# Seven PSUM banks instead of three for one more attention head, and for the norm before it

## The chip, the cores and the metric

One core of one Trainium2 chip runs the whole program. The metric is device time in microseconds (us) of one execution. Engines are named as in the profile: PE (TensorE, matmuls), PEld (its weight loads), DVE (VectorE), ACT (ScalarE), POOL (GpSimd), SP (the queue that issues the DMAs). PSUM is the memory that PE writes its results to. This kernel cuts it into eight tiles of 128 x 512 float32, called banks below: four named `pm`, three named `ps`, one named `po`.

## The reference

```python
# attention, 4 batches x 8 heads, 576 positions, 64 wide, mask by blocks of 64
scores = scale * q @ k.T; scores = where(block_i >= block_j, scores, -1e9)
attn = exp(scores - max); attn = attn / (sum + 1e-9)
x = (attn @ v), heads side by side                      # 2304 tokens x 512
# gated feed-forward ("MoE 1"), 512 -> 1536 -> 512
xn = x / sqrt(mean(x * x) + 1e-6) * rms_g
x = (silu(xn @ w_gate) * (xn @ w_val)) @ w_out
# mixture of 8 experts ("MoE 2"), 512 -> 1024 -> 512, with a weight P for each token and expert
P = exp(x @ gate - max); 8 rounds of scaling its rows and columns
out = sum over e of P[:, e] * (relu(x @ w1[e]) @ w2[e])
```

## The kernel before

Heads are numbered 0 to 31 (head i is head i % 8 of batch i // 8), so head 8 opens the second batch and "the second batch's second head" is head 9. The Python code first writes a graph of operations, in program order; `Graph.emit` then plans twelve orders for all engines with estimated durations and keeps the best. What the program order fixes for good is the use of buffers: each `Ring` hands out its tiles in turn, and an operation on a newly drawn tile waits for everyone who used that tile before.

`attention` runs heads as a software pipeline. Its step i makes, in turn, the scores of head i and the second half of head p = i - 1:

- `s_a` to `s_d` (matmuls L504): four score blocks, one bank each; DVE takes negated row maxima (L513, combined in L554), ACT the exponentials (L520). The longest rows span two banks, so `s_c` and `s_d` are both held until the exponentials after `s_d`.
- `s_norm` (DVE L671 and L672, ACT L679 or DVE L681): scales the rows by one over their sums.
- `t_x0` to `t_x3` (heads from 7 on): PE transposes the weights (L689) into one bank each; ACT (L695) and DVE (L696) take a high and a low part out.
- `pv_a` to `pv_d` (L729): products with v into the single `po` bank, the last 64 columns into the bank of `t_x3`; ACT (L754) copies one half to a `tm` tile, DVE (L757) adds the other.

Heads 0 to 6 use another form of the second half, also with four banks a head. So each head draws eight banks from the ring `ps_ring[0]`.

After the last head of a batch comes its norm. `rms_a` sums squares with ten tiny matmuls (L792) into a first bank; DVE takes the inverse root there (L796 to L802) and spreads it on a diagonal (L809); PE broadcasts it (L818) into a bank for 512 tokens and one for the last 64. For the first batch these banks are read straight by `rms_b`: eight multiplications on DVE (L877, four of 512 and four of 64 columns), each followed by a copy to a high part (ACT, L294) and a subtraction for the low part (POOL or DVE, L307). Their `tm` tiles come from a ring of three, shared with `pv_d`. For later batches the banks are copied out first (L827).

Only a batch that has its norm can feed MoE 1 (matmuls L959 up, L1015 down, on the `pm` banks). `attention` is a generator: at each `yield` the caller adds some groups of MoE 1 to the graph, four groups for the first batch's tokens at the first `yield`. PE then mixes their matmuls with the attention of later batches.

Banks pass from one use to the other so. At first `PS0`, a ring of seven, serves attention: ps0, pm0, ps1, pm1, ps2, pm2, pm3. Heads 0 to 8 with their scores and heads 0 to 7 with their second halves draw 68 times from it. Then `PS` (three banks) serves attention, and `PM` (four) serves MoE 1; `PS.after = PM.after = PS0` makes the first draws of both wait for the users of `PS0` on the same tile. The first batch's norm draws its three banks from `PM`.

Other helpers in the rows: L294, L298 and L300 are copies that split off high parts, L307 the subtractions for low parts, L350 to L356 the conversion of weights, L474 a step of loading a head, L662 the end of a head in the other form, L765 and L777 the squares and their sum.

Of the kernel before, what the change touches and what calls it, by code (L numbers as in the profile page):

```python
# [197 lines left out]
def t_act(n, psum=False, ap=0):  # L198
    if ALONE:
        return (165 if psum else 190) + 0.845 * n + 144 * ap  # L200
    return (50 if psum else 92) + n / 1.2 + 90 * ap
# [17 lines left out]
def t_v2(n):  # L219
    return Both(150 + n / 1.92) if ALONE else 120 + n / 0.96  # L220
# [10 lines left out]
def t_f32(n):  # L231
    return 2 * max(n / 1.2, 107.0) + 2
# [3 lines left out]
def tile_attn_moe_moe2(ctx: ExitStack, tc: tile.TileContext, qT, kT, vP, wg, wv, wo, rg, gw, w1, w2, ident_d, mq_d, mk_d, bm_d, out):  # L236
    nc = tc.nc
    B, H, D, S = qT.shape
# [18 lines left out]
    def tiles(pool, n, shape, dt, name):  # L257
        return [pool.tile(shape, dt, name=f"{name}{i}") for i in range(n)]
# [17 lines left out]
    PM = Ring(tiles(psp, 4, [128, 512], F32, "pm"))  # L276
    PS = Ring(tiles(psp, 3, [128, 512], F32, "ps"))
# [4 lines left out]
    ps_ring = [PS0]  # L282
# [119 lines left out]
    def A(*a, **k):  # L402
        k.setdefault("prio", 1.0)
        o = G.op(*a, **k)
        att_ops.append(o)
        return o
# [40 lines left out]
    def att_load(i):  # L447
        b, h = divmod(i, H)
        Rqa, Rqb, Rka, Rkb, Rrq = (*b0_rings, RQ0) if i < H else (QA, QB, KA, KB, RQ)
        qb, kb = Rqb.next(), Rkb.next()  # L450

        def load_two(b_, src):
            def ld():
                nc.sync.dma_start(out=b_()[0:64], in_=src[b, h])
                nc.sync.dma_start(out=b_()[64:128], in_=src[b, h])
            A("SP", 1200, ld, w=[b_], lat=2000)

        if H <= i < H + 2:

            clear = st["clear", i % 2] = qb.part()  # L460
            A("DVE", 300, lambda: nc.vector.memset(f32(qb()[96:128, :]), 0.0), w=[clear])
        qq, kk = Rrq.next(), Rrq.next()
        load_two(kk, kT)
        load_two(qq, qT)
        qa, ka = Rqa.next(), Rka.next()
        sc = 1.0 if i in NEW else scale
        copy(A, S, ka, kk, r=[kk], w=[ka])
        copy(A, S, lambda: qa()[:, PAD:640], qq, sc, r=[qq], w=[qa])
        copy(A, S, lambda: qb()[0:64, PAD:640], lambda: qq()[0:64], sc, r=[qq], w=[qb])
        minus(A, S, lambda: kb()[0:64], lambda: kk()[0:64], lambda: f32(ka()[0:64]), r=[kk, ka], w=[kb], margin=GAIN)  # L470
        if i in NEW:
            minus(A, S, lambda: qa()[64:128, PAD:640], lambda: qq()[64:128], lambda: f32(qa()[64:128, PAD:640]), r=[qq, qa], w=[qa], margin=GAIN)
        else:
            A("DVE", 120 + t_v1(S), lambda: nc.vector.scalar_tensor_tensor(  # L474
                out=qa()[64:128, PAD:640], in0=qq()[64:128], scalar=scale, in1=f32(qa()[64:128, PAD:640]), op0=ALU.mult, op1=ALU.subtract),
                r=[qq, qa], w=[qa])
        st["in", i] = (qa, qb, ka, kb)

    def att_open(i):
        b, h = divmod(i, H)  # L480
        st["m", i], st["sm", i] = MN.next(par=True), SM.next(par=True)
        st["P", i] = [p.next(par=True) for p in PP]
        if i not in NEW and i < H + 1:
            for t in (0, 3):
                p = st["P", i][t]
                A("POOL", 150, lambda p=p, t=t: nc.gpsimd.memset(p()[:, NKEY[t] :], 0.0), w=[p])
        if i in NEW:
            vx = st["vs", i] = VX.next()

            def ldv():  # L490
                nc.sync.dma_start(out=vx()[:, 0:4, D : 2 * D], in_=vP[b, h][:, 0:4])
                nc.sync.dma_start(out=vx()[64:128, 4, D : 2 * D], in_=vP[b, h][0:64, 4])

            A("SP", 1200, ldv, r=[vones], w=[vx], lat=2000)
            return
        vr, vs = RV.next(), VS.next()
        st["vs", i] = vs
        A("SP", 700, lambda: nc.sync.dma_start(out=vr(), in_=vP[b, h]), w=[vr], lat=2000)
        copy(A, 320, lambda: vs()[:, :, 0:D], vr, r=[vr], w=[vs])
        minus(A, 320, lambda: vs()[:, :, D : 2 * D], vr, lambda: f32(vs()[:, :, 0:D]), r=[vr, vs], w=[vs], margin=GAIN2)  # L500
# [281 lines left out]
    def rms_a(b):  # L782


        ring = PM if b == 0 else ps_ring[0]
        ss, ps, c = st.pop(("ss", b)), ring.next(), CL.next()
        V = nc.vector
        at = [min(128 * t, S - 128) for t in range(5)]

        def sums():  # L790
            for t in range(5):
                nc.tensor.matmul(out=ps()[:, t : t + 1], lhsT=ss()[:, at[t] : at[t] + 128], rhs=ones_t[:, 0:1], start=True, stop=True)  # L792

        def newton():
            m, t, y = ps()[:, 8:13], ps()[:, 16:21], c()
            V.tensor_scalar(out=m, in0=ps()[:, 0:5], scalar1=1.0 / DM, scalar2=1e-6, op0=ALU.mult, op1=ALU.add)  # L796
            V.tensor_scalar(out=t.bitcast(I32), in0=m.bitcast(I32), scalar1=1, scalar2=None, op0=ALU.logical_shift_right)
            V.tensor_scalar(out=y.bitcast(I32), in0=t.bitcast(I32), scalar1=-1, scalar2=0x5F3759DF, op0=ALU.mult, op1=ALU.add)
            for _ in range(3):
                V.tensor_tensor(out=t, in0=y, in1=m, op=ALU.mult)  # L800
                V.scalar_tensor_tensor(out=t, in0=t, scalar=-0.5, in1=y, op0=ALU.mult, op1=ALU.mult)
                V.scalar_tensor_tensor(out=y, in0=t, scalar=1.5, in1=y, op0=ALU.add, op1=ALU.mult)  # L802

        A("PE", 1200, sums, r=[ss, ones, mask], w=[ps], prio=0.0)
        A("DVE", 2500, newton, r=[ps], w=[c])
        dg = SS.next(par=True)
        for t in range(5):
            n = min(128, S - 128 * t)
            A("DVE", 63 + t_v2(n), lambda t=t, n=n: V.tensor_scalar_mul(  # L809
                out=dg()[:, 128 * t : 128 * t + n], in0=ident_t[:, 128 - n : 128], scalar1=c()[:, t : t + 1]), r=[c, ident], w=[dg], prio=0.9)  # L810
        spreads = []
        for o, n in ((0, 512), (512, S - 512)):
            y = ring.next()

            def spread(y=y, o=o, n=n):
                for k in range(0, n, 128):
                    w = min(128, n - k)
                    nc.tensor.matmul(out=y()[:, k : k + w], lhsT=ones_t, rhs=dg()[:, o + k : o + k + w], start=True, stop=True)  # L818

            A("PE", t_f32(n), spread, r=[dg, ones], w=[y], prio=0.0)  # L820
            spreads.append((o, n, y))
        if b == 0:
            st["y", b] = [(o, o + n, y) for o, n, y in spreads]
        else:
            ys = SS.next(par=True)
            for o, n, y in spreads:
                A("ACT", t_act(n, True), lambda o=o, n=n, y=y: nc.scalar.activation(  # L827
                    out=ys()[:, o : o + n], in_=y()[:, 0:n], func=AF.Copy), r=[y], w=[ys], prio=0.9)
            st["y", b] = [(0, S, ys)]
# [62 lines left out]
    def attention():  # L892

        att_init()
        att_load(0)
        att_open(0)
        A("SP", 300, lambda: nc.sync.dma_start(out=ident_t, in_=ident_d), w=[ident], lat=2000)
        A("SP", 100, lambda: nc.sync.dma_start(out=rg_t, in_=rg), w=[rgs], lat=2000)
        def nothing(i):
            pass  # L900

        old = ((t_x0, nothing), (t_x1, pv_a), (t_x2, pv_b), (t_x3, pv_c), (nothing, pv_d))
        new = ((st_a, nothing), (st_b, sv_a), (st_c, sv_b), (st_d, sv_c), (nothing, sv_d))
        for i in range(NH + 1):
            p = i - 1
            for s, (x, y) in zip((s_a, s_b, s_c, s_d, s_norm), new if p in NEW else old):
                if i < NH:
                    s(i)
                if p >= 0:
                    y(p)  # L910
                    x(p)
            if i + 1 < NH:
                att_load(i + 1)
                att_open(i + 1)
            if p >= 0:
                b, h = divmod(p, H)
                if h % 2:
                    sq_step(b, h // 2)
                if h == H - 1:
                    rms_a(b)  # L920
                    rms_b(b)
                    if b == 0:
                        ps_ring[0] = PS
                        b0_ops.update(*(x.users for x in (bm, vones, *VX, *M10, *SR, *RC, *RQ0)))
                    yield


# [768 lines left out]
```

## Time and profile before

| | |
|---|---|
| median of 3 runs | 2183.27 us (2181.48 to 2185.68) |
| profiled execution | 2186.54 us, of which the span from first to last instruction is 2184.8 us |
| mean granted clock of PE | 0.989 of full speed |
| busy share of the span | PE 98%, PEld 85%, DVE 64%, POOL 53%, ACT 44% |

The busy shares are means over phases with different limits: attention fills the first 470 us or so, and MoE 1 and 2 the rest. Attention of the second batch overlaps the first batch's MoE 1 from about 106 us on. A mean clock of 0.5 in a stretch is PE's lower level (1.2 GHz), 1.0 the higher (2.4 GHz).

### The profile page before, as it was taken

To read this page: it belongs to the slowest core of one execution; us is meant where nothing else is said; L and a number is where in the kernel's file an instruction comes from. 1 tells how busy PE (TensorE), PEld (TensorE's weight loads), DVE (VectorE), ACT (ScalarE), POOL (GpSimd) and SP (SyncE) were. 2 spreads that over 40 slices of the span, in tenths; PEclk is the share of its full clock that TensorE was granted. 3 is DMA by queue.
4 is the path that set the end of the run, shared out by engine and by line. 5 is a ranking of instruction groups with operands and counts; after the bars stand their busy time and mean duration, and the time that the engine had idled before them with its cause. 6 is when DMAs were issued, how large, how long until landed. Compare 5 with 4: busy or idle time off the path is not lost.

```text
span 2184.8 us, 31245 instructions
## 1 busy us (share of the span) xinstructions
PE 2145.4 (98%) x10974; PEld 1859.9 (85%) x10974; DVE 1402.8 (64%) x2396; ACT 967.2 (44%) x2118; POOL 1160.9 (53%) x1079
## 2 busy tenths in 40 slices
PE   8899999999999999999999999999999999999999
PEld 5677788888999998999999999899888888888887
DVE  6789887863633577555555555555676677767666
ACT  6888786661421543333343433433343333233332
POOL 6556446311522666665565565565465556465554
PEclk9799999999999999999999999999999999999999
DMA  5666667635775544555545555555666566556663
GB/s 158 191 192 215 214 201 242 196 128 185 241 248 203 209 177 175 193 183 178 174 174 185 182 183 185 187 181 175 208 202 194 201 202 200 197 200 205 193 201 116
DMA packets 160976, 419.20 MB, mean 192 GB/s; under 512 B 22298, under 2 KB 52826, under 8 KB 160820
## 3 DMA queue, kind: packets, MB, share of 16 engines
q1 hardware_dynamic: 160820, 417.22, 57.2%
q8 instruction: 86, 1.41, 0.3%
q14 instruction: 70, 0.57, 0.1%
HBM read 274.74 MB, written 141.08 MB: 190 GB/s over the span
## 4 chain that ended last, share of the span: by engine, by line
PE 83%; DVE 2%; ACT 1%; POOL 1%; issue 1%; POOLq 0%; DVEq 0%; ACTq 0%
PE ps L1359 25%; PE pm L1427 20%; PE pm L1584 11%; PE pm L959 9%; PE pm L1359 7%; PE pm L1015 5%; PE po L1584 3%; PE ps L689 1%; PE po L729 1%; PE ps L504 1%; PE po L974 0%; DVE qa L474 0%; DVE xs L307 0%; DVE mn L513 0%; DVE acc L1443 0%
## 5 line engine op out<-in xcount | busy, mean ns | idle before, releaser
L1359 PE MATMUL ps<-xs,w 128*128 128x384 f32 (+2 forms) x2478 | 505.5, 346 | 2.2 <-ACT t L1369 1.2
L1359 PEld LDWEIGHTS ps<-xs,w 128*128 128x128 f32 x2478 | 435.7, 188 | 46.4 <-ACT t L1369 1.9
L959 PE MATMUL pm<-x,w 128*128 128x512 f32 (+1 forms) x1440 | 341.2, 378 | 0.0
L1443 DVE SCALAR_TENSOR_TENSOR acc<-pm,Pm,acc 128x512 f32<-128x512 f32 x280 | 209.7, 750 | 162.2 <-PE pm L1427 159.0
L1427 PE MATMUL pm<-w,h 128*128 128x512 f32 x1152 | 279.1, 391 | 0.0
L959 PEld LDWEIGHTS pm<-x,w 128*128 128x128 f32 x1440 | 254.4, 190 | 28.3
L307 POOL TENSOR_TENSOR w<-raw,w 128x512 fp32r<-128x512 f32 (+1 forms) x163 | 195.0, 1206 | 105.0 <-ACT w L294 96.4
L1427 PEld LDWEIGHTS pm<-w,h 128*128 128x128 f32 x1152 | 210.0, 188 | 39.7
L1427 PE MATMUL pm<-w,x 128*128 128x512 f32 x768 | 186.8, 392 | 0.0
L307 POOL TENSOR_TENSOR h<-t,h 128x512 fp32r<-128x512 f32 (+1 forms) x64 | 80.1, 1251 | 182.4 <-ACT h L294 169.8
L1565 DVE TENSOR_TENSOR acc<-pm,acc 128x512 f32<-128x512 f32 x169 | 116.5, 690 | 81.1 <-PE pm L1584 80.4
L1427 PEld LDWEIGHTS pm<-w,x 128*128 128x128 f32 x768 | 143.1, 188 | 26.9
L1015 PE MATMUL pm<-h,w 128*128 128x512 f32 (+1 forms) x720 | 162.8, 375 | 0.0
L1015 PEld LDWEIGHTS pm<-h,w 128*128 128x128 f32 x720 | 131.1, 190 | 16.0
L1374 DVE TENSOR_TENSOR pad<-ps,pad 128x384 f32<-128x384 f32 (+2 forms) x127 | 66.3, 522 | 114.1 <-ACT pad L1369 72.0
L1359 PE MATMUL pm<-xs,w 128*128 128x256 f32 (+2 forms) x654 | 139.1, 336 | 0.0
L307 POOL TENSOR_TENSOR w<-pad,w 128x512 fp32r<-128x512 f32 x64 | 88.6, 1386 | 71.3 <-ACT w L294 71.3
L1584 PE MATMUL pm<-x,w 128*128 128x512 f32 x510 | 125.6, 389 | 0.5 <-DVE x L307 0.5
L1359 PEld LDWEIGHTS pm<-xs,w 128*128 128x128 f32 x654 | 112.2, 189 | 14.7
L307 POOL TENSOR_TENSOR x<-pad,x 128x512 fp32r<-128x512 f32 (+1 forms) x71 | 94.7, 1337 | 54.1 <-ACT x L294 54.1
L1369 ACT ACTIVATE pad<-ps 128x256 f32<-128x256 f32 (+2 forms) x115 | 55.0, 478 | 140.1 <-PE ps L1359 140.0
L1584 PEld LDWEIGHTS pm<-x,w 128*128 128x128 f32 x510 | 95.7, 188 | 20.7 <-DVE x L307 0.9
(365 smaller groups left out, 4140.6 us busy)
## 6 DMA issues: line engine op xcount, KB each, us to landing
raw<-w_dram SPq DMA_DIRECT2D x128, 256.0 KB, 3.0
w<-kg SPq DMA_DIRECT2D x48, 512.0 KB, 4.1
w<-kv SPq DMA_DIRECT2D x48, 512.0 KB, 3.5
w<-ko SPq DMA_DIRECT2D x48, 512.0 KB, 4.0
fa<-w SPq DMA_DIRECT2D x32, 512.0 KB, 4.3
fd<-w SPq DMA_DIRECT2D x32, 512.0 KB, 3.9
fc<-w SPq DMA_DIRECT2D x32, 512.0 KB, 2.9
sb<-w SPq DMA_DIRECT2D x32, 512.0 KB, 3.8
```

The source lines that it names most:

```text
L307: eng.tensor_tensor(out=out_(), in0=a(), in1=b(), op=ALU.subtract)
L504: nc.tensor.matmul(out=ps()[:, o : o + n], lhsT=a[:, 128 * t : 128 * t + 128], rhs=c[:, k0 : k0 + n], start=start, stop=stop)
L689: A("PE", 109, lambda: nc.tensor.transpose(out=ps()[:, o : o + 128], in_=p()[:, 128 * c : 128 * c + 128], identity=ident_t), r=[p, ident, ...
L959: nc.tensor.matmul(out=ps()[:, 0:n], lhsT=w()[:, a, 128 * k : 128 * k + 128], rhs=xv()[:, c, k, 0:n], start=k == 0 and (a, c) == (0, 0), s ...
L1015: nc.tensor.matmul(out=ps()[:, 0:n], lhsT=wos[q]()[:, a, 128 * m : 128 * m + 128], rhs=ht()[:, c, 0:n], start=q == 0 and (a, c) == (0, 0), ...
L1359: nc.tensor.matmul(out=bank()[:, 0:n], lhsT=w()[:, a, o + 128 * k : o + 128 * k + 128], rhs=views[p, q, i, k, c](), start=start and k == 0 ...
L1369: G.op("ACT", t_act(n, True), lambda: nc.scalar.activation(out=t()[:, 0:n], in_=bank()[:, 0:n], func=AF.Copy), r=[bank], w=[t])
L1374: G.op("DVE", t_v1(n), lambda: nc.vector.tensor_tensor(out=t()[:, 0:n], in0=bank()[:, 0:n], in1=t()[:, 0:n], op=ALU.add), r=[bank, t], w=[t])
L1427: nc.tensor.matmul(out=y(), lhsT=hs[f][half]()[:, a, o : o + 128], rhs=ws[f]()[:, c, :], start=f == 0 and (a, c) == (0, 0), stop=f == GF - ...
L1443: G.op("DVE", 63 + t_v1(512), lambda y=y, dst=dst, tt=tt, e=e: nc.vector.scalar_tensor_tensor(out=dst(), in0=wide(y()), scalar=Pm()[:, tt, ...
L1565: G.op("DVE", t_v1(N), lambda: nc.vector.tensor_tensor(out=dst(), in0=bank()[:, 0:N], in1=dst(), op=ALU.add), r=[bank, dst], w=[dst])
L1584: nc.tensor.matmul(out=bank()[:, 0:N], lhsT=w()[:, a, o : o + 128], rhs=ops[i][gi]()[:, c, 0:N], start=start and gi == 0 and (a, c) == (0, ...
```

## The change

`rms_a` draws its banks from whatever ring attention uses at the time, for the first batch too. The switch to three banks, and with it the first `yield`, moves from the end of the step with p = 7 to the end of the step with p = 8.

```diff
     def rms_a(b):
...
-        ring = PM if b == 0 else ps_ring[0]
+        ring = ps_ring[0]
         ss, ps, c = st.pop(("ss", b)), ring.next(), CL.next()
...
                     rms_a(b)
                     rms_b(b)
                     if b == 0:
-                        ps_ring[0] = PS
                         b0_ops.update(*(x.users for x in (bm, vones, *VX, *M10, *SR, *RC, *RQ0)))
+                    else:
+                        yield
+                elif p == H:
+                    ps_ring[0] = PS
                     yield
```

So after 68 draws the seven-bank ring goes on for eleven more: three for the norm, then the scores of head 9 in turn with the second half of head 8. Counted through the ring: norm pm2, pm3, ps0; `s_a` pm0, `t_x0` ps1, `s_b` pm1, `t_x1` ps2, `s_c` pm2, `t_x2` pm3, `s_d` ps0, `t_x3` pm0. Before the change these eight were ps0, ps1, ps2, ps0, ps1, ps2, ps0, ps1, and the norm had pm0, pm1, pm2. No instruction is added or taken away.

## Rows read from the trace of the kernel before

**Rows 1.** The page: busy tenths of PE and its clock in 40 slices.
```profile
PE   8899999999999999999999999999999999999999
...
PEclk9799999999999999999999999999999999999999
```
**Rows 2.** Busy time by stretch: PE, PEld, DVE, ACT, POOL, then clock and DMA.
```profile
86.50:106.50 20.00, 16.62 (x63) 14.13 (x62) 15.38 (x41) 15.90 (x39) 12.95 (x10) 0.50 0.60 204
...
106.00:215.00 109.00, 103.79 (x534) 85.06 (x532) 100.84 (x189) 93.41 (x233) 69.62 (x56) 0.96 0.63 199
215.00:230.00 15.00, 11.55 (x49) 9.59 (x48) 12.69 (x27) 6.55 (x18) 7.66 (x7) 0.77 0.72 249
230.00:470.00 240.00, 235.95 (x1257) 196.74 (x1256) 191.03 (x393) 183.65 (x469) 99.04 (x90) 1.00 0.61 198
```
**Rows 3.** PE in order of time: start, length, instruction, [idle before].
```profile
84.56 0.63 PE L504 MATMUL ps<-ka,qa 128*128 128x320 f32 x1 [2.49 <-DVE xx L757]
...
85.63 1.91 PE L689 MATMUL ps<-ident,p 128*128 128x128 f32 x8
...
88.74 0.79 PE L504 MATMUL ps<-ka,qa 128*128 128x512 f32 x1
...
90.18 0.26 PE L504 MATMUL ps<-ka,qa 128*128 128x64 f32 x1
...
90.98 1.05 PE L689 MATMUL ps<-ident,p 128*128 128x128 f32 x4
...
92.21 2.13 PE L792 MATMUL pm<-ones,ss 128*128 128x1 f32 x10
...
98.00 0.93 PE L689 MATMUL ps<-ident,p 128*128 128x128 f32 x2 [2.56 <-ACT p L679]
98.72 1.91 PE L818 MATMUL pm<-ss,ones 128*128 128x128 f32 x8
...
106.09 2.75 PE L959 MATMUL pm<-x,w 128*128 128x512 f32 x9
...
113.56 0.39 PE L729 MATMUL po<-pth,vs 128*128 128x512 f32 x1
...
209.19 1.17 PE L792 MATMUL ps<-ones,ss 128*128 128x1 f32 x10
```
**Rows 4.** DVE in order of time, the same stretch.
```profile
84.28 0.22 DVE L757 TENSOR_TENSOR xx<-ps,tm 64x64 f32<-64x64 f32 x1
...
94.37 0.17 DVE L796 TENSOR_SCALAR pm<-pm 128x5 f32<-128x5 f32 x1 [2.31 <-PE pm L792]
...
96.68 0.16 DVE L671 TENSOR_REDUCE rs<-sm 128x5 f32<-128x15 f32 x1
...
100.67 0.75 DVE L877 SCALAR_TENSOR_TENSOR tm<-xx,rgs,pm 128x512 f32<-128x512 f32 x1 [0.42 <-PE pm L818]
...
110.98 0.56 DVE L877 SCALAR_TENSOR_TENSOR tm<-xx,rgs,pm 128x64 f32<-128x64 f32 x2 [0.18 <-POOL x L307]
112.25 0.53 DVE L300 TENSOR_SCALAR qa<-rq 128x576 fp32r<-128x576 f32 x1 [0.71 <-PE ps L504]
...
113.37 4.08 DVE L300 TENSOR_SCALAR qb<-rq 64x576 fp32r<-64x576 f32 x1
```
**Rows 5.** ACT in order of time.
```profile
80.91 0.73 ACT L520 ACTIVATE p<-pm,mn 128x512 f32<-128x512 f32 x1
...
102.73 0.62 ACT L294 ACTIVATE x<-tm 128x512 fp32r<-128x512 f32 x1
...
109.25 0.60 ACT L754 ACTIVATE tm<-po 64x512 f32<-64x512 f32 x1
```
**Rows 6.** POOL in order of time.
```profile
89.04 1.43 POOL L777 TENSOR_TENSOR ss<-ss,tm 128x576 f32<-128x576 f32 x1 [1.06 <-DMA kv<-w]
...
103.43 1.27 POOL L307 TENSOR_TENSOR x<-tm,x 128x512 fp32r<-128x512 f32 x1 [0.64 <-ACT x L294]
...
115.84 1.29 POOL L356 TENSOR_TENSOR raw<-acc 128x512 int32<-128x512 int32 x1
```

## The prediction

> **What bounds the kernel now.** I read the page first: PE is at nine tenths or more in all slices but the first two, and only the second, which holds the place of the change, has a low clock [rows 1]. Then the busy time by stretch [rows 2]. From 230 us on PE is nearly gapless (235.95 of 240 us busy, full clock), so what happens there is paid in matmuls, and the change adds none. What it can move is the PE time lost before: the norm of the first batch (86.5 to 106.5 us, PE at the lower clock level throughout, 3.4 us idle), the overlap of the second batch's attention with MoE 1 (106 to 215 us, 5.2 us idle), and the wait for the second batch's norm (215 to 230 us, 3.45 us idle, mean clock 0.77). In that last stretch PE has run out of MoE work that may start, so a delay or gain of the second batch's attention reaches the end of the kernel as it is. The overlap stretch is DVE's more than PE's: DVE 100.84 of 109 us.
>
> Last I followed each engine in order of time through the norm [rows 3 to 6]. The reader should see two things. First, a bank wait: head 9's `s_b` starts at 84.56, 2.49 us late, released by the DVE addition at 84.28 that ends head 7 [rows 3, 4]; it draws the tile that head 7's `t_x3` had. Over the 20 us from 86.5 PE's clock is at the lower of its levels (0.50) [rows 2]. Second, the norm is one long chain with attention squeezed between its links: POOL completes the sum of squares at 89.04 + 1.43 = 90.47 [rows 6], PE starts the tiny matmuls only at 92.21, DVE gets them at 94.37, PE broadcasts at 98.72, DVE multiplies at 100.67, ACT copies at 102.73, POOL subtracts until 103.43 + 1.27 = 104.70, and MoE 1 starts at 106.09.
>
> **The change, part by part.** The instructions are the same; only the tiles differ, and so the waits.
>
> *Head 9's first two blocks.* `s_b` moves to pm1, last used by head 8's `s_d`, whose exponentials follow those of `s_c` (80.91 + 0.73) [rows 5]: some 82 us instead of 84.56. `s_a`, which before ran earlier than `s_b`, must now wait for pm0, which head 8's `s_c` holds to 81.64. So the 2.49 us wait goes, but the next PE work, the eight transposes at 85.63 [rows 3], needs head 8's scaled rows and no bank. I count 0 for this; bounds 0 and -2.5 us.
>
> *Head 9's last blocks and head 8's `t_x2` get the norm's banks.* This is the dear part. `s_c` (88.74 before) must wait until DVE is done with pm2 (94.37 to about 96.7); `t_x2` (90.98 before) until the four 512-column multiplications have read pm3; `s_d` (90.18 before) until the four 64-column ones have read ps0, and their last pair ends at 110.98 + 0.56 = 111.54 before [rows 3, 4]. Queued behind `s_d` are head 9's maximum, its exponentials, `s_norm` (96.68 before), its transposes (98.00 before), and head 10's `s_a`, whose ps0 is `s_d`'s. PE's part of all this runs after MoE 1 has begun, no longer in time that PE would lose anyway. The three 512-column matmuls between 88.74 and 90.18 take 0.48 us each at the lower level, so 0.24 at the higher, 0.47 ns a column. Pushed out are `s_c`, `s_d` (2 x 576 columns), head 10's `s_a` (2 x 512) and head 8's `pv_c`, `pv_d` (2 x 640): 3456 columns, 1.6 us; and three times four transposes, at half of 1.05 us each, 1.6 us. Together +3.2 us; bounds 0 (they fit into gaps after 106 us, 5.2 us in all) and 3.2.
>
> *The norm loses its company.* With those out of the way its links close up. The tiny matmuls can start at 90.5 instead of 92.21: 1.7 us. The broadcast stands behind head 9's transposes from 98.00 to 98.72: 0.7. ACT's first copy comes 1.3 us after the multiplication's end (100.67 + 0.75 = 101.42; copy at 102.73), because the evacuation of head 9's transposes was ahead of it in ACT's queue. MoE 1 starts 1.4 us after its first operand is there (104.70 to 106.09), with attention before it on PE. Sum -5.1 us, so MoE 1 near 101 us; bounds 0 (other work is planned into the holes) and -5.1. MoE's own banks do not take this back: the first gate product draws pm0, which head 8's `pv_d` frees late, but the first value product draws pm1, free early, and the planner knows both.
>
> *The attention path.* Head 8's end does not wait for banks alone: ACT's copy at 109.25 needs a `tm` tile, and those are drawn after the norm's eight [rows 5]. If the norm ends 5 us earlier, this copy can too, even with `t_x2` late. Head 9: the last 64-column read would be at 111.5 - 5.1 = 106.4; then scores, maxima, exponentials, scaling and transposes. In the kernel before, `s_d` at 90.18 was followed by the first transposes at 98.00, 7.8 us; from 106.4 that gives 114.2, and the evacuation 115, against `pv_a` of head 9 at 113.56 [rows 3]. PE's clock is back by then and the shorter latencies give about half a us back: I take +1 us of lag at the second batch's norm; bounds -3 us (the idle time in 215 to 230, about all that a faster attention can win there) and +6 us (nothing gained by the norm: 111.5 + 7.8 = 119.3 against 113.56).
>
> One price in this depends on where things land. A DVE copy of 64 x 576 elements took 4.08 us at 113.37, where the larger one at 112.25 took 0.53; it ended at 117.45, just after POOL's row that ends at 115.84 + 1.29 = 117.13 [rows 4, 6]. A catch-up of attention that meets such a row costs up to 3.5 us; I put it into the high end only. The Trainium skill (SBUF — State Buffer, section "Who interferes with whom") says that GpSimd and a VectorE copy share one port pair as an exclusive lock, and the second to come blocks fully; the trace agrees with its 4.08 us, and by that rule bunching the norm's POOL subtractions beside DVE's copies speaks against the change.
>
> **The sum.** 0 + 3.2 - 5.1 + 1 = -0.9 us. The profiled execution took 2186.54 us (span 2184.8 plus 1.7 around it) and would come to 2185.6. It lies 3.3 us above the median of the runs; on the median the same sum gives 2182.4 us. About 0.2%, 4.4 us, is what a measurement of this kernel can tell from no change.
>
> **The rivals.**
>
> *A: the terms cancel* (my forecast, 0.43): -4 to +4 us, 2179 to 2187.5 us. For it: the norm's chain stays a chain of the same instructions, and what leaves the norm comes back after it.
>
> *B: slower* (0.28). The norm's banks are held long and attention stands still meanwhile. Place: `s_d` of head 9 on ps0, and `t_x2` of head 8 on pm3. It decides from where the last 64-column read comes later than about 107 us, i.e. where the norm wins less than 4.5 us. At the extreme the norm wins nothing: +3.2 + 6 = +9 us, 2192.5; at its middle +6, 2189. For it: DVE's 92% in the overlap leaves little to catch up with. Against it: the evidence that head 8's end waited for the norm anyway.
>
> *C: faster* (0.29). The norm wins its 5.1 us, the pushed-out matmuls fit into gaps, and the attention path leads instead of lagging: -5.1 + 0 to -5.1 - 2.5, with the 3 us of idle before the second norm as the source; about -6 us, 2177. For it: PE's rows of 88 to 94 us are back to back at the lower level, so the tiny matmuls do wait for the queue. Against it: in the wait for the norm PE has nothing else to do, so a lead is worth only what the following stretches can use. The Trainium skill (Perfetto Trace Analysis, section "Matmul Optimizations") asks that all eight PSUM banks be used for parallelism; by this rule the change should gain, and the trace shows one wait of 2.49 us that agrees with it and a norm that would hold three of the banks, which does not.
>
> *D: it does nothing by itself*, within A: another order comes out of the planner's twelve rounds, and a few us either way are chance.
>
> **The numbers.** Forecast 2182.4. The ends are C's middle with 1 us to spare and B's upper part: 2176 to 2191; A alone is 2179 to 2187.5. Faster by over 0.2% has C's 0.29, within 0.2% A's 0.43, slower B's 0.28.
>
> **What would show it.** Right: `s_b` of head 9 without its 2.5 us wait; the `ps` score matmuls of head 9 now on `pm`; tiny matmuls within 0.3 us of the sum's end; `s_d` of head 9 right behind the last 64-column multiplication; first MoE matmul at 101 to 102 us; the second norm's tiny matmuls within 2 us of where they were (209.19 us) [rows 3]. Wrong: MoE 1 starting after 106 us (B), or the second norm's stretch without idle PE (C). I would be wrong altogether if PE's idle time changed after 230 us, where I count nothing, or if the orders there were replanned so that a wait appears in MoE 2.

## The result, and the profile after

| | before | after |
|---|---|---|
| median of 6 runs on one chip | 2184.42 us (2181.48 to 2187.52) | 2195.41 us (2191.63 to 2200.75) |
| ratio | | 1.0053 [1.0041, 1.0065] |
| profiled execution, its span | 2186.54, 2184.8 us | 2200.75, 2199.0 us |
| mean granted clock of PE | 0.989 | 0.988 |

The change costs 11 us, 0.5%. The forecast was 2182.4 us and the range ended at 2191. The direction is that of rival B, and the size is beyond its extreme. The profiled execution after is the slowest of its six, 5.3 us above their median, so its own difference of 14.2 us to the profile before says a little too much.

The page of the kernel after, busy tenths and clock of PE in 40 slices:

```profile
PE   8699999999999999999999999999999999999998
...
PEclk9799999999999999999999999999999999999999
```

Against [rows 1] the second slice has gone from 8 to 6 tenths. Next, busy time by stretch of the kernel after, with the columns of [rows 2]:

```profile
106.00:150.00 44.00, 38.32 (x175) 30.19 (x176) 36.63 (x65) 32.67 (x84) 24.90 (x23) 0.88 0.56 185
150.00:205.00 55.00, 51.66 (x275) 41.40 (x274) 47.25 (x95) 50.26 (x128) 32.08 (x25) 0.97 0.58 188
205.00:235.00 30.00, 26.09 (x126) 20.84 (x125) 29.34 (x55) 21.96 (x52) 21.57 (x17) 0.95 0.68 216
...
235.00:480.00 245.00, 241.26 (x1274) 200.92 (x1273) 192.56 (x401) 185.49 (x477) 101.52 (x91) 0.99 0.62 201
```

The same stretches of the kernel before:

```profile
106.00:150.00 44.00, 40.63 (x205) 33.46 (x203) 39.73 (x71) 36.45 (x93) 30.78 (x27) 0.95 0.62 196
150.00:205.00 55.00, 53.16 (x280) 43.28 (x281) 51.30 (x105) 52.17 (x132) 31.80 (x24) 0.97 0.66 202
```

Busy time times clock is PE's work in microseconds at full speed. From 106 to 150 us that is 38.32 x 0.88 = 33.7 after, against 40.63 x 0.95 = 38.6 before: 4.9 us lost, part by idling and part because the granted clock fell. From 150 to 205 us it is 50.1 against 51.6, another 1.5 us. In the first of the two stretches PE, DVE, ACT and POOL all did less, so none of them had become the bound.

Part of this is only a shift: head 7's first transpose, ahead of which no bank differs, stands at 74.09 us before and at 78.71 after. Counted from there, the two stretches of the kernel after are these:

```profile
110.71:154.71 44.00, 39.20 (x188) 31.55 (x188) 34.31 (x63) 34.39 (x89) 22.20 (x21) 0.88 0.52 164
154.71:209.71 55.00, 51.79 (x275) 41.88 (x274) 49.65 (x99) 50.29 (x131) 33.35 (x25) 0.97 0.58 180
```

That is 34.5 and 50.2 us of work, so 4.1 and 1.4 us less than before. From 235 us on PE is nearly gapless again.

PE of the kernel after in order of time, as in [rows 3]:

```profile
94.07 0.74 PE L504 MATMUL pm<-ka,qa 128*128 128x448 f32 x1 [4.43 <-ACT p L520]
...
95.94 2.13 PE L792 MATMUL pm<-ones,ss 128*128 128x1 f32 x10
...
101.57 0.63 PE L504 MATMUL pm<-ka,qa 128*128 128x512 f32 x1
...
102.42 1.07 PE L818 MATMUL pm<-ss,ones 128*128 128x128 f32 x8
...
106.09 0.50 PE L962 MATMUL pm<-x,w 128*128 128x512 f32 x1 [0.79 <-ACT x L294]
...
108.24 0.66 PE L689 MATMUL pm<-ident,p 128*128 128x128 f32 x4
...
112.47 0.19 PE L504 MATMUL ps<-ka,qa 128*128 128x64 f32 x1
...
120.62 0.93 PE L689 MATMUL ps<-ident,p 128*128 128x128 f32 x2 [2.98 <-ACT p L679]
121.21 1.63 PE L962 MATMUL pm<-x,w 128*128 128x512 f32 x3
...
126.33 0.48 PE L729 MATMUL po<-pth,vs 128*128 128x512 f32 x1
...
221.41 1.28 PE L792 MATMUL ps<-ones,ss 128*128 128x1 f32 x10 [0.25 <-POOL ss L777]
```

These rows are head 9's `s_a`, the norm's tiny matmuls, head 9's `s_c`, the broadcast, the first MoE 1 matmul, head 8's `t_x2`, head 9's `s_d`, its first transposes, a MoE 1 group of three matmuls behind them, its `pv_a`, and the second norm. `s_a` waits 4.43 us on pm0 for head 8's exponentials. `s_d` went from 90.18 to 112.47 us, `pv_a` from 113.56 to 126.33, and the second norm from 209.19 to 221.41.

DVE of the kernel after, as in [rows 4]:

```profile
98.14 0.16 DVE L796 TENSOR_SCALAR pm<-pm 128x5 f32<-128x5 f32 x1
...
111.56 0.56 DVE L877 SCALAR_TENSOR_TENSOR tm<-xx,rgs,ps 128x64 f32<-128x64 f32 x2 [0.47 <-POOL x L307]
...
114.57 3.35 DVE L300 TENSOR_SCALAR qb<-rq 64x576 fp32r<-64x576 f32 x1
117.95 1.71 DVE L474 SCALAR_TENSOR_TENSOR qa<-rq,qa 64x576 fp32r<-64x576 f32 x1
119.69 0.17 DVE L671 TENSOR_REDUCE rs<-sm 128x5 f32<-128x15 f32 x1
```

ACT and then POOL of the kernel after, as in [rows 5] and [rows 6]:

```profile
115.37 0.20 ACT L520 ACTIVATION_READ_ACCUMULATOR p<-ps,mn 128x1 f32 x1
...
120.12 2.13 ACT L679 ACTIVATE p<-p,rs 128x192 f32<-128x192 f32 x4 [3.44 <-DVE rs L672]
...
125.08 0.59 ACT L1000 ACTIVATE t<-pm 128x512 f32<-128x512 f32 x1
```
```profile
116.32 1.28 POOL L307 TENSOR_TENSOR w<-raw,w 128x512 fp32r<-128x512 f32 x1
```

The last two reads of the 64-column bank end at 111.56 + 0.56 = 112.12, and `s_d`, whose bank ps0 that is, follows at 112.47. Its exponentials are done at 115.37 + 0.20 = 115.57. But the reduction with which the scaling of the rows begins comes only at 119.69: DVE had taken on a 64 x 576 copy of 3.35 us and a load step of 1.71 us first. PE stands 2.98 us before the transposes at 120.62.

### The profile page after: what moved, and what is told of

The parts are those of the page before. It is cut to its first block, busy times and chain, and to the rows that moved or that the text cites. A ratio compares the mean times of both kernels' runs of the same rounds, so it can differ in the third digit from the quotient of the medians.

```text
span 2199.0 us, 31270 instructions
## 1 busy us (share of the span) xinstructions
PE 2147.4 (98%) x10974; PEld 1859.1 (85%) x10974; DVE 1408.4 (64%) x2395; ACT 966.9 (44%) x2119; POOL 1158.4 (53%) x1079
## 4 chain that ended last, share of the span: by engine, by line
PE 88%; DVE 7%; ACT 2%; issue 1%; POOL 1%; DMA 0%; SPq 0%; ACTq 0%; DVEq 0%; POOLq 0%
PE ps L1362 24%; PE pm L1430 19%; PE pm L962 11%; PE pm L1587 11%; PE pm L1362 7%; PE pm L1018 6%; PE po L1587 3%; PE ps L689 1%; PE ps L504 1%; PE po L729 1%; DVE qa L474 1%; ACT p L679 1%; DVE mn L513 1%; PE po L618 1%; DVE ptl L696 1%
## 5 line engine op out<-in xcount | busy, mean ns | idle before, releaser
L962 PE MATMUL pm<-x,w 128*128 128x512 f32 (+1 forms) x1440 | 347.0, 381 | 1.7 <-POOL x L307 0.9
L1362 PEld LDWEIGHTS pm<-xs,w 128*128 128x128 f32 x654 | 112.1, 189 | 14.7
L1372 ACT ACTIVATE pad<-ps 128x256 f32<-128x256 f32 (+2 forms) x115 | 54.9, 477 | 141.2 <-PE ps L1362 141.1
```

The lines of the kernel that those rows point to most:

```text
L962: nc.tensor.matmul(out=ps()[:, 0:n], lhsT=w()[:, a, 128 * k : 128 * k + 128], rhs=xv()[:, c, k, 0:n], start=k == 0 and (a, c) == (0, 0), s ...
L1362: nc.tensor.matmul(out=bank()[:, 0:n], lhsT=w()[:, a, o + 128 * k : o + 128 * k + 128], rhs=views[p, q, i, k, c](), start=start and k == 0 ...
L1372: G.op("ACT", t_act(n, True), lambda: nc.scalar.activation(out=t()[:, 0:n], in_=bank()[:, 0:n], func=AF.Copy), r=[bank], w=[t])
```

## The experiments

The planner chooses a new order for every graph, so a change of banks is a change of order too. In what follows, **old order** and **new order** mean that each operation gets its place in the plan of the kernel before, or after, as its priority, and its engine fixed; the times of the two original kernels are those of their own plans. The common measure of lag is the time from head 7's first transpose to the first tiny matmul of the second norm. All kernels run the same number of matmuls ahead of that transpose (289), and none differs in a bank there; the kernels in the old order run them in the same sequence, the others in sequences of their own. The column "head 7 to end" is the time from the same transpose to the end of the span. Ratios are to the kernel before on the same chip; lags and times to the end come from one profile each.

| kernel | banks | order | head 7's transpose, us | second norm, us | lag, us | head 7 to end, us | median, us | ratio |
|---|---|---|---|---|---|---|---|---|
| before | old | old | 74.09 | 209.19 | 135.1 | 2110.7 | 2184.42 | 1 |
| after | new | new | 78.71 | 221.41 | 142.7 | 2120.3 | 2195.41 | 1.0053 |
| e1 | new | old | 78.91 | 228.92 | 150.0 | 2117.0 | 2197.08 | 1.0052 [1.0039, 1.0066] |
| e2 | old | new | 75.11 | 211.70 | 136.6 | 2107.5 | 2186.61 | 1.0006 [0.9998, 1.0015] |
| e3 | old | own, round 9 | 70.74 | 201.66 | 130.9 | 2107.8 | 2177.74 | 0.9975 [0.9967, 0.9983] |
| e4 | new | own, round 9 | 80.06 | 211.25 | 131.2 | 2106.8 | 2188.90 | 1.0023 [1.0014, 1.0031] |
| e5 | old | own, round 6 | 74.55 | 211.75 | 137.2 | 2111.0 | 2187.20 | 1.0011 [1.0002, 1.0019] |
| e6 | new | own, round 3 | 81.97 | 213.01 | 131.0 | 2106.8 | 2190.46 | 1.0030 [1.0019, 1.0041] |
| g1 | new, copied out | old | 76.97 | 221.02 | 144.1 | 2117.2 | 2195.29 | 1.0047 [1.0034, 1.0059] |
| g2 | new, norm drawn last | old | 72.53 | 213.62 | 141.1 | 2115.8 | 2190.84 | 1.0034 [1.0022, 1.0046] |
| g3 | norm's ring alone | old | 75.20 | 222.97 | 147.8 | 2115.6 | 2192.79 | 1.0035 [1.0022, 1.0048] |
| g4 | four, none of the norm's | old | 74.97 | 208.94 | 134.0 | 2107.3 | 2184.94 | 1.0004 [0.9996, 1.0013] |
| k1 | as g4 | own | 77.20 | 213.71 | 136.5 | 2109.9 | 2190.34 | 1.0025 [1.0016, 1.0035] |
| h1 | g4, `s_c` waits | old | 78.84 | 213.47 | 134.6 | 2108.7 | 2185.36 | 1.0003 [0.9993, 1.0014] |
| h2 | g4, `t_x2` waits | old | 72.47 | 206.43 | 134.0 | 2107.5 | 2186.19 | 1.0002 [0.9991, 1.0013] |
| h3 | g4, `s_d` waits | old | 76.97 | 219.58 | 142.6 | 2109.3 | 2186.39 | 1.0015 [1.0007, 1.0024] |
| h5 | g4, `t_x2`, `s_d` wait | old | 71.15 | 212.99 | 141.8 | 2110.4 | 2186.32 | 1.0014 [1.0003, 1.0024] |
| h4 | g4, all three wait | old | 77.47 | 223.05 | 145.6 | 2117.5 | 2198.23 | 1.0068 [1.0055, 1.0080] |
| h7 | as h5 | new | 75.20 | 213.12 | 137.9 | 2106.8 | 2187.78 | 1.0016 [1.0007, 1.0025] |
| h6 | as h4 | new | 75.17 | 214.77 | 139.6 | 2106.9 | 2187.22 | 1.0011 [1.0002, 1.0020] |

The times from head 7's transpose to the end fall into two groups: 2115.6 to 2120.3 us for the kernel after, e1, g1, g2, g3 and h4, and 2106.8 to 2111.0 us for all others, e4 and e6 with the new banks among them.

### Banks or order: e1 and e2

e1 is the changed kernel in the old order, e2 the kernel before in the new order. The edit of both (the table is that of the other kernel's plan):

```diff
-        best = None
-        for r in range(ROUNDS):
-            order, end = self.forward()
...
-        for fn in best[1]:
-            fn()
...
+        for pos in range(len(table) // 2):
+            o = seq[table[2 * pos] % 2][table[2 * pos] // 2]
+            o.key, o.alts = (pos, 0), [o.alts[table[2 * pos + 1]]]
+        for o in self.forward()[0]:
+            o.fn()
```

> The changed kernel (new banks, new place of the yield), but its planner is replaced by one pass in which every operation has its place in the order of the kernel before as its priority, on the engine that it had there; so the two programs are alike up to head 9, and differ only as far as the banks force it. Theory 'banks' (the norm's three banks hold up heads 8 and 9, whatever the order): 2190 to 2196 us, second norm's tiny matmuls at 216 us or later. Theory 'order' (the loss is the new order that the planner made of the whole program, of which 4.6 us are already lost at head 7's transposes, 78.71 us instead of 74.09, where no bank differs): 2181 to 2188 us, second norm within 4 us of 209.2.

> The kernel before with the order of the changed kernel as priorities, the reverse of the run above. Theory 'banks': within 3 us of the kernel before, about 2184 us. Theory 'order': 2189 to 2196 us, and head 7's transposes at about 78.7 us as in the changed kernel.

Measured 1.0052 and 1.0006. The new banks cost 0.52% in the old order and 0.47% in the new one, the new order by itself 0.01 to 0.06%. So in these two orders the loss goes with the banks. e1 shows it in the stretch after the norm: in the 44 us that begin 32 us after head 7's transpose (at 78.91 us in e1, 74.09 before) its PE did 41.34 x 0.82 = 33.9 us of work, against 38.6 before. That is 4.7 us less; from head 7's transpose to the end e1 takes 6.3 us more. Busy time of e1:

```profile
110.91:154.91 44.00, 41.34 (x187) 34.13 (x188) 31.46 (x65) 34.27 (x86) 23.36 (x21) 0.82 0.47 152
```

PE of e1 in order of time:

```profile
87.22 0.72 PE L504 MATMUL pm<-ka,qa 128*128 128x448 f32 x1
...
101.06 0.80 PE L504 MATMUL pm<-ka,qa 128*128 128x512 f32 x1 [2.49 <-DVE cl L802]
...
106.31 0.79 PE L962 MATMUL pm<-x,w 128*128 128x512 f32 x1 [1.18 <-ACT x L294]
...
113.37 1.05 PE L689 MATMUL pm<-ident,p 128*128 128x128 f32 x4
...
117.41 0.31 PE L504 MATMUL ps<-ka,qa 128*128 128x64 f32 x1
...
228.92 1.17 PE L792 MATMUL ps<-ones,ss 128*128 128x1 f32 x10
```

DVE of e1, the last two norm reads of the 64-column bank:

```profile
115.58 0.46 DVE L877 SCALAR_TENSOR_TENSOR tm<-xx,rgs,ps 128x64 f32<-128x64 f32 x2
```

With the old order the holds stand bare: `s_c` waits 2.49 us for the norm's inverse root, `t_x2` comes at 113.37 and `s_d` at 117.41 instead of 90.98 and 90.18. The 4.43 us wait of `s_a` seen after is not there (87.22, no idle before it), so e1 loses as much without it; whether it carries a part of the loss in the new order is not shown.

### Other orders of both graphs: e3, e4, e5, e6

The planner makes twelve rounds and keeps one. These kernels take another round of the same graph (e3 and e4 round 9, e5 round 6, e6 round 3):

```diff
-            if best is None or end < best[0]:
+            if r == 9:
```

> The kernel before with another of its planner's twelve plans (the one of round 9 instead of round 2, which the planner likes next best), nothing else. It shows how much another order alone moves the time. Theory 'order': 4 us or more away from the kernel before, on either side. Theory 'banks': within 3 us.

> The changed kernel with another of its planner's plans (round 9 instead of round 2). Theory 'banks': it stays at 2192 us or more. Theory 'order': anything from 2183 to 2198 us, 4 us or more away from the changed kernel's 2195.4.

> The kernel before with a third plan of its planner (round 6). Theory 'banks': 2177 to 2189 us, in a cloud with the other two plans (2177.7 and 2184.4). Theory 'scatter': it can come out as slow as the changed kernel, 2190 us or more.

> The changed kernel with a third plan of its planner (round 3). Theory 'banks': 2188 us or more, with the others (2188.9 and 2195.4). Theory 'scatter': it can come out at 2184 us or less.

Four orders with the old banks gave 0.9975, 1, 1.0006 and 1.0011 (mean 0.9998); four with the new ones 1.0023, 1.0030, 1.0052 and 1.0053 (mean 1.0040). The two sets don't overlap and their means lie 0.42%, 9 us, apart. The order alone moves either graph by 0.3% or more. e3 is the fastest kernel of the study, 0.25% under the kernel before, with no change of banks at all. e4, at 2188.90 us, missed the 2192 us or more that theory 'banks' asked for.

But for e4 and e6 the loss does not stand where the banks differ. Their head 7 transposes at 80.06 and 81.97 us, later than in any other kernel of the table (70.74 to 78.91), and from there to the end they take 2106.8 us, less than the four with the old banks (2107.5 to 2111.0). Both profiles lie within 0.3 us of their kernel's median. Yet `s_d` is held in them as in the kernel after. DVE's last norm reads and then PE's `s_d` in e4:

```profile
112.27 0.56 DVE L877 SCALAR_TENSOR_TENSOR tm<-xx,rgs,ps 128x64 f32<-128x64 f32 x2 [0.47 <-POOL x L307]
```
```profile
113.19 0.19 PE L504 MATMUL ps<-ka,qa 128*128 128x64 f32 x1
```

That is 33.1 us after head 7's transpose, against 33.8 in the kernel after (112.47 less 78.71). So the hold by itself does not make the loss, and in two of the four orders the new banks show no cost after head 7, as far as one profile each can tell.

### Which hold: g1, g2, g3, g4

The edits shown from here on are to the kernel after, where nothing else is said; the old order is put on as in e1.

g1 lets the first batch's norm copy its broadcast banks out, as later batches do, so that the multiplications no longer hold pm3 and ps0:

```diff
-        if b == 0:
-            st["y", b] = [(o, o + n, y) for o, n, y in spreads]
+        if False:
+            pass
```

> New banks with the old order as priorities (as the first run), and the first batch's norm, like that of the later batches, copies its two broadcast banks out with two ACT copies, so that pm3 and ps0 come free some 0.6 us after the broadcast instead of after the last of eight multiplications. Theory 'held' (heads 8 and 9 stand still behind the norm's hold on pm3 and ps0): 2184 to 2189 us, most of the loss gone. Theory 'handover' (the loss is that MoE 1 gets its first bank, pm0, only when head 8 has ended, or simply starts later): no better than 2193 us.

1.0047 against 1.0052 of e1: no difference that these intervals can tell, although `s_norm` of head 9 came at 109.53 us instead of 121.58. So a shorter time of reading does not buy the loss back here. But g1 adds a delay of its own: MoE 1 starts at 110.80 us, 33.8 after head 7's transpose, against 27.4 in e1. A bank drawn early for the norm is also out of use until the sums arrive; that this is why is argued, not shown.

g2 draws the norm's three banks after head 9's step instead of ahead of it:

```diff
                 if h == H - 1:
-                    rms_a(b)
-                    rms_b(b)
...
                 elif p == H:
+                    MODE[0] = 2; rms_a(0), rms_b(0); MODE[0] = 1
...
                     ps_ring[0] = PS
```

> As the first run, but in program order the first batch's norm stands behind head 9's step, so head 9 draws its eight banks first and the norm the three after them; heads 8 and 9 wait for the norm no more. Theory 'held': 2181 to 2187 us. Theory 'handover': 2193 us or more, since MoE 1 still gets its banks after head 9 and the norm's last bank is now pm0.

1.0034: about a third comes back, though the interval overlaps that of e1. By the turn of the rings the hold has moved on: the norm's banks are now the next ones of head 10's `s_a` (ps0) and of MoE 1 (pm0).

g3 makes the first hunk of the diff alone. The norm draws pm2, pm3 and ps0, and attention goes to three banks where it did before. Against the kernel before:

```diff
-        ring = PM if b == 0 else ps_ring[0]
+        ring = ps_ring[0]
```

> Half of the change alone, old order as priorities: the norm draws from the ring of seven (pm2, pm3, ps0), but the switch to three banks and the yield stay where they were, so that head 9's first block is the one that waits for ps0. Theory 'held': 2188 to 2197 us, as bad as the whole change or worse, since head 9 starts behind the norm. Theory 'handover': within 3 us of the kernel before.

1.0035 and a lag of 147.8 us: about two thirds of the loss without any of the extra banks for head 9. Here head 9's `s_a` draws ps0 and stands behind the norm's 64-column reads.

g4 is the counterpart: head 9 gets a fourth bank, pm3, but none of the norm's, which are pm0 to pm2 again; the `yield` stays at its new place:

```diff
-    PS.after = PM.after = PS0
+    P4, N3 = Ring([*PS.tiles, PM.tiles[3]]), Ring(PM.tiles[:3])
+    P4.after, N3.after, PS.after, PM.after = PS0, PS0, Chain(P4), Chain(N3, P4)
...
-        ring = ps_ring[0]
+        ring = N3 if b == 0 else ps_ring[0]
...
                     if b == 0:
+                        ps_ring[0] = P4
```

> The other half as nearly as it can be had alone, old order as priorities: the norm keeps three banks of its own (pm0 to pm2, as before), and head 9 with head 8's second half draws from the four others (ps0, ps1, ps2, pm3) before attention goes over to three; the yield is one step later, as in the change. Theory 'held': 2180 to 2186 us, no loss, since nobody in attention waits for the norm. Theory 'handover': 2190 us or more.

1.0004 and a lag of 134.0 us: nothing lost, and nothing won by the extra bank or the later `yield`. With the planner free the same graph came to 1.0025:

> The four-bank version with the planner making its own order for it: the norm on pm0 to pm2, head 9 on the other four, the yield one step later. Both theories: 2177 to 2186 us, at least level with the kernel before, since it has one bank more for head 9 and none of the change's waits; over 2190 us would mean that something else in the change costs.

The 2190.34 us are just past the 2190 that the expectation had set as a sign of another cost. From head 7's transpose to the end k1 takes 2109.9 us, within the range of the old banks, so no cost of its own shows there; where its excess stands was not followed further.

Of the two theories, g3 and g4 bear out 'held' and g1 'handover', while g2 lies between the two. Neither explains all four.

### One wait at a time: h1 to h5

To g4, where no attention bank is the norm's, each of these adds a wait that the change had made. h1 lets head 9's `s_c` wait for the users of the norm's first bank, h2 head 8's `t_x2` for the 512-column reads, h3 head 9's `s_d` for the 64-column reads; h5 has the last two and h4 all three:

```diff
         ps2, ps, m = st.pop(("s2", i)), ps_ring[0].next(), st["m", i]
+        if i == H + 1:
+            ps.before |= N3[2].users
         s_mm(i, ps, 0, 4, 512, 64)
```

> The four-bank kernel, in which nothing in attention waits for the norm, with one wait of the change put back: head 9's third score block waits until the first batch's norm is done with its first bank (the inverse root). Theory 'sum' (each of the three waits has its price): 2185 to 2188 us. Theory 'last block' (only the fourth block's wait counts, since head 9's maximum hangs on it): 2184 us, as the four-bank kernel. Theory 'transposes' (only head 8's wait counts, since the single po bank and head 9's products are behind it): 2184 us.

> The four-bank kernel with the second wait alone: head 8's third group of transposes waits until the four 512-column multiplications of the norm have read their bank. Theory 'transposes': 2191 us or more. Theory 'sum': 2186 to 2189. Theory 'last block': 2184 to 2186.

> The four-bank kernel with the third wait alone: head 9's fourth score block waits until the four 64-column multiplications of the norm have read theirs. Theory 'last block': 2191 us or more. Theory 'sum': 2187 to 2190. Theory 'transposes': 2184 to 2186.

> The four-bank kernel with all three waits. If they are the loss of the change, the time is that of the first run with the change's banks and the old order, 2193 to 2198 us; if it stays under 2190, something else of the seven-bank ring (pm0, which head 9's first block and MoE 1's first product share with head 8) has a part.

> The four-bank kernel with two waits put back: head 8's third transposes behind the 512-column multiplications and head 9's fourth block behind the 64-column ones; head 9's third block is free. Theory 'together' (one late head leaves the other's work to fill in, two leave none): 2193 us or more, as with all three. Theory 'scatter' (the prices just add and the run with all three was an unlucky order): 2186 to 2189 us.

The lag answers clearly. `s_c` and `t_x2` add nothing (134.6 and 134.0 us against 134.0 in g4), `s_d` adds 8.6 us. PE of g4 and then of h3 in order of time, head 9's `s_d` and the second norm:

```profile
91.63 0.28 PE L505 MATMUL ps<-ka,qa 128*128 128x64 f32 x1
...
208.94 1.17 PE L793 MATMUL ps<-ones,ss 128*128 128x1 f32 x10
```
```profile
113.21 0.19 PE L505 MATMUL ps<-ka,qa 128*128 128x64 f32 x1
...
219.58 1.17 PE L795 MATMUL ps<-ones,ss 128*128 128x1 f32 x10
```

The time does not follow in proportion. h3 and h5 are slower than g4 by 0.11 and 0.10%, some 2.3 us for 8 us of lag, and their intervals overlap that of g4; by the expectations h5 falls into the range of 'scatter'. All three waits together add 0.64%, 14 us, for 11.6 us of lag. So in the old order the three waits together make a loss as large as the whole of e1's, and no single one or tested pair accounts for it. Busy time of g4 and then of h4 shows where, in the stretches from 32 to 76 and from 76 to 131 us after head 7's transpose:

```profile
106.97:150.97 44.00, 40.62 (x210) 31.75 (x209) 40.78 (x75) 37.36 (x96) 29.20 (x25) 1.00 0.63 196
150.97:205.97 55.00, 52.53 (x275) 41.72 (x274) 50.91 (x101) 50.60 (x127) 33.13 (x26) 1.00 0.68 215
```
```profile
109.47:153.47 44.00, 40.94 (x209) 33.00 (x210) 35.46 (x71) 37.54 (x95) 26.52 (x24) 0.95 0.54 164
153.47:208.47 55.00, 50.12 (x258) 40.69 (x257) 50.64 (x97) 48.76 (x125) 27.76 (x22) 0.94 0.56 181
```

PE's work falls from 40.6 to 38.9 us in the first stretch (40.94 x 0.95) and from 52.5 to 47.1 in the second (50.12 x 0.94), 7.1 us in all, three quarters of it well after the waits themselves are over.

### The same waits in the new order: h6, h7

> The four-bank kernel with all three waits, with the changed kernel's order as priorities instead of the old one. Theory 'third block decides' (with head 9's third block late as well, attention has nothing left to fill in): 2193 us or more again. Theory 'order' (2198 us was an unlucky order): 2185 to 2191 us.

> The four-bank kernel with the two late waits only, with the changed kernel's order as priorities. Theory 'third block decides': 2184 to 2189 us again, at least 5 us under the run beside it. Theory 'order': within 3 us of the run beside it.

The edits are those of h4 and h5; only the order is the new one. Measured 1.0011 and 1.0016, against 1.0068 and 1.0014 in the old order. So the three waits that cost 14 us in one order cost next to nothing in the other, as theory 'order' had it, while the full change costs 0.47% there. What the full change has beyond these waits is that MoE 1's banks come free later: pm0 is head 8's until its end, pm2 head 9's until its exponentials. That was not tried alone. The first tanh of MoE 1 doesn't speak for it as the one cause: it comes 47.9 us after head 7's transpose in h6, which loses 0.11%, and 37.8 us after it in g3, which loses 0.35%.

## Why the prediction was wrong

**The bank wait (0).** Right in size: the 2.49 us of `s_b` are gone, `s_a` waits for pm0 instead, and e1, where neither waits, is as slow as the kernel after.

**"Head 9's last blocks and head 8's `t_x2`" (+3.2).** That they came late is borne out by the rows above; the price of the pushed-out matmuls is shown by no run by itself.

**"The norm loses its company" (-5.1).** The sum of the chain said a first MoE matmul near 101 us and a last 64-column read at 106.4; measured were 106.09, as before, and 112.1. Counted from head 7's transpose MoE 1 starts 27.4 us on in the kernel after, against 32.0 before. In the old order the banks alone do this (27.4 in e1), so 4.6 of the 5.1 us came there; but e1's last 64-column read ends at 115.58 + 0.46 = 116.04 us, 37.1 after head 7's transpose against 37.5 before, and that read is what `s_d` waits for. In the new order the start moves by 0.6 us (28.0 in e2). In neither order did it win time. My links closed up on paper only: in the kernel after `s_c` at 101.57 still runs between the tiny matmuls and the broadcast.

**"The attention path" (+1, bounds -3 and +6).** This is the step that failed: the lag of the second batch's attention was mis-sized, and its upper bound with it. The second norm moved by 12.2 us in the two profiles; counted from head 7's transpose the lag grew by 7.6 us there, by 6.1 between e2 and the kernel after, and by 14.9 in the old order (135.1 to 150.0). Less the 74.09 us of head 7's transpose, the sum had the last read at 32.3 us (106.4), the first transposes at 40.1 (114.2) and the evacuation before `pv_a` at 40.9 (115); the kernel after has 33.4, 41.9, and `pv_a` at 47.6. So the chain behind `s_d` was nearly right, and most of what was missing lies between the first transposes and `pv_a`, 5.7 us instead of under 1, where PE runs groups of MoE 1 (as at 121.21) between one transpose and the next. In e1 the last read itself came late (37.1), and `pv_a` stands at 49.3 (128.18). The mechanism stood in rival B (`s_d` on ps0), and h3 shows that this wait by itself makes 8.6 us of lag; `t_x2`, which B named beside it, makes none. B's point of decision, a last 64-column read later than about 107 us, was passed by 5 us (0.5 us counted from head 7's transpose, 4.2 in e1). What B did not say is that the same hold can cost nothing, as in e4, e6 and h6.

**"Reaches the end of the kernel as it is."** Wrong both ways. h3's 8.6 us of lag cost 2.4 us against g4 (within the intervals); g3's 12.7 us over the kernel before cost 7.7; e1's 14.9 cost 11.4; the kernel after lags 6.1 us behind e2 and loses some 10. Part of a lag can be made up for behind the second norm: from it to the end e1 takes 1967.0 us (2195.9 less 228.92), the kernel before 1975.6. And PE can lose work long after the wait, as the row of h4 from 153.47 us shows; that a late attention leaves it less to mix in would fit, but is not shown.

**The port price ("into the high end only").** It did land: the 64 x 576 copy took 3.35 us and ended at 117.92, behind POOL's row that ends at 116.32 + 1.28 = 117.60, and it stood between head 9's exponentials and its scaling. The Trainium skill (SBUF — State Buffer, section "Who interferes with whom") has the engine that comes second block on a lock; the trace agrees with its 3.35 us, against 0.44 us for another copy of this size at 89.56, where POOL had no work. Not every overlap does this: e2's copy at 107.89 took 0.44 us beside POOL's subtractions (104.74 to 108.51). g4 and h6 have slow copies too (4.49 and 4.14 us) and lose next to nothing, and e1 lost as much without one at this place: from `s_d` to the reduction of `s_norm` it took 4.2 us there (117.41 to 121.58), 7.2 in the kernel after (112.47 to 119.69) and 6.5 in the kernel before (90.18 to 96.68). So this is not the cause of the loss in the old order; what it costs in the kernel after is not shown.

**"MoE's own banks do not take this back."** Its first tanh went from 113.48 to 125.08 us, 39.4 to 46.4 counted from head 7's transpose. The banks were late; what that cost stays open, as said above.

**D, the planner's chance.** "A few us either way" was right for the pair at hand (0.01 to 0.06%), but too small in general: e3 gains 0.25%, e4 and e6 seem to lose by their order alone, and h4 and h6, the same graph, differ by 0.57%.

Of the signs listed, `s_b` without its wait, head 9's scores on `pm` and `s_d` right behind the last 64-column multiplication came true. The tiny matmuls (1.2 us behind the sum's end at 93.29 + 1.48 = 94.77), the start of MoE 1 and the second norm did not. After the second norm little moved, as forecast: 1975.6 us to the span's end before, 1977.6 after.

Rival C, faster, did not come either: g4's extra bank is worth nothing that can be told (1.0004 [0.9996, 1.0013]).

Settled is that the bank assignment costs about 0.5% in the old and in the new order, that in the old order the norm's draw from attention's ring is enough for most of it (g3), the extra bank without it is harmless (g4), and the three waits together make a loss of that size (h4). Not settled is the cause in general: the same hold of `s_d` costs nothing after head 7 in e4, e6 and h6. Open is what in an order decides this, and what makes up the loss in the kernel after.

## What to carry to other kernels

More banks can be worth nothing. Here they won nothing without the norm in the ring (g4), and with it they cost 0.5% in two orders. The ring hands out its banks in turn: whoever draws next behind a slow chain (here a norm) waits for its last read, and its own chain queues behind that. What such a wait costs depended here on the order of everything else, from nothing to 14 us. So ask who draws the slow chain's banks next. And where a planner reorders everything, compare several of its orders on each side before believing 0.3%, and look whether the difference stands where the change is: that of e4 and e6 stood ahead of it.

## What was not expected of the hardware

In the eleven kernels whose matmuls stand in the same order up to head 7's first transposes, the profiles show these between 71.15 (h5) and 78.91 us (e1), 74.09 in the kernel before. The granted clock differs in the stretches before it, as in this row of e1 and then of the kernel before:

```profile
20.00:30.00 10.00, 10.00 (x41) 6.84 (x40) 4.29 (x12) 5.77 (x13) 5.45 (x5) 0.79 0.38 109
```
```profile
20.00:30.00 10.00, 10.00 (x47) 7.02 (x46) 4.14 (x12) 6.61 (x17) 7.07 (x6) 0.91 0.48 141
```

PE is busy throughout in both, and at 0.79 instead of 0.91 it does less in that time. Why the clock differs is open; it means that two single profiles of this kernel that stand up to 8 us apart in place say nothing about a change, and it is why lags and stretches are counted from head 7 here.
